# Sixteen score tiles moved forward, and one exponential moved behind a copy, in a fused attention and MLP kernel

## The chip, the cores and the metric

The kernel runs on one core of a Trainium2 chip. The metric is the device time in microseconds; the median of three runs before the change was 1639.81 us (1639.73 to 1642.65). The core has five engines with queues of their own: TensorE (PE, with its weight loads PEld), VectorE (DVE), ScalarE (ACT), GpSimd (POOL) and SyncE (SP), which here only issues DMAs. PE writes its results to PSUM, which is divided into eight banks; a tile of 128 x 512 float32 fills one bank.

## The reference

```python
xn = _layernorm(x)                                   # x: 1 x 2048 x 512
q, k, v = split(xn @ wqkv)                           # 32 heads of 16
scores = einsum("bhqd,bhkd->bhqk", q, k) * 16**-0.5
s = (softmax(scores) @ v) @ wo
g = silu(gelu(xn @ w1 + b1) @ w2 + b2)               # 512 -> 1376 -> 512
return x + s * g
```

There are 2048 tokens, a model width of 512, 32 heads of 16, and a hidden width of 1376. The inputs are float32.

## The kernel before

The products are made in float32 accuracy from two parts: an operand is split into a rounded part and a rest (names ending in h and l), and three products, hh, hl and lh, are summed in one PSUM bank.

**Units and tiles.** Attention is cut into 32 units. A unit `u` is a group of four heads (`g = u // 4`, `NG` = 8 groups) with a chunk of 512 queries (`c = u % 4`). Each unit is computed twice. The first pass makes 64 *score tiles* of 128 queries by 512 keys (`s_one`, line 165): a matmul (line 174) and a row maximum by DVE (line 176). They serve only to find each query's maximum. When a unit's 64 tiles are done, `s_end0`, `s_end1` and `s_end2` negate, transpose and store the maxima to DRAM. The second pass makes the *probability tiles*, 128 keys by 512 queries (`t_one`, line 647): a matmul (line 654) whose operands carry two additional rows, so that the maximum is subtracted within the product, and an exponential by ACT (line 656). The *value product* (`pv_step`, line 716, matmuls on line 723) accumulates 16 key blocks of a unit in one bank, and after the last one ACT copies the bank out to SBUF (the output copy, `os`, line 730).

**Three stages.** The first (to about 53 us) normalises and transposes x and computes part of the values and the queries and keys of groups 0 and 1. The queries and keys go to DRAM (`qk_h`, `qk_l`, lines 312 and 313) and come back with their rows rearranged (`load_k`, line 99, and `load_qs`, line 133).

The second stage, the *MLP stage* (to about 479 us), runs a list of parts (`plan`): the rest of the values (`quad`), the two MLP products (`half` and `down`) and the remaining queries and keys. All its matmuls contract over 64 rows, two halves of PE's rows working side by side; `run` walks through slots of two such matmuls, and `prog["n"]` counts them. Between them `fill` (line 481) puts early score tiles, by a due count that is linear in the slot number: it starts at slot `FILL0` = 84 and reaches `4 * LEAD` = 560 tiles at the last of `SLOTS` = 1470 slots. Loads for later units stand on a list, `errands`; one entry is taken at fixed places of each `half`. The weights' loads and the list's loads share SP's queue.

The third stage, the *attention stage*, is a loop of 513 steps written out by hand. Step n makes the four probability tiles T of key block n % 16 of unit n // 16, some score tiles S of later units, and the value product V of the step before. How many S there are is the difference of a due count (line 839) and the tiles already made; their place in the step is a string:

```python
ORDER = {0: "TTTTV", 1: "TTTTSV", 2: "TTTSTSV", 3: "STTTSTSV", 4: "STTSTSVTS"}
...
return min(4 * L, 4 * LEAD + max(0, (4 * (L - LEAD) * n - 300) // (DONE - 1)))
```

`L` is 512, and `DONE` = 492 is the step from which the output projection is worked in.

**Banks in the attention stage.** The four T of a step write the bank of `ps_m` and the three of `ps_t`, in that order (`t_tile`, line 639). The S use two banks of `ps_s` and a third, which alternates: `ps_v` and `ps_x` take turns as accumulator of the value product, and the one that isn't accumulating serves score tiles. At step 16u + 1 the ring of score banks is set anew: the first two S take `ps_s`, the third takes the bank of the unit that has just ended.

**Hand-over.** Step 16u holds the first four T of unit u and the last value product of unit u - 1. In the order in which ACT gets its work, the four exponentials come first and the output copy after them.

**Keys.** Three buffers hold keys (`KB` = 3). Group 3 reuses the first buffer: POOL's queue issues its loads in two halves of 1024 keys, at steps 57 and 64. Later groups are loaded piece by piece.

Of the kernel before, what the change touches and what calls it, by code (L numbers as in the profile page):

```python
# [10 lines left out]
AF = mybir.ActivationFunctionType  # L11
# [6 lines left out]
S = 2048  # L18
# [5 lines left out]
CH = 512  # L24
NCH = S // CH
# [4 lines left out]
EPS = 1e-5  # L30
SCALE = DH ** -0.5
VW = DH + 1
LEAD = 140
NW = 10
EARLY = 4
DONE = 492
FILL0 = 84
HB = 4
W2B = 2
ORDER = {0: "TTTTV", 1: "TTTTSV", 2: "TTTSTSV", 3: "STTTSTSV", 4: "STTSTSVTS"}  # L40
KB = 3
# [5 lines left out]
def fused(ctx: ExitStack, tc: tile.TileContext, x, wqk, wv, wo, w1, b1, w2, b2, out):  # L47
    nc = tc.nc
# [50 lines left out]
    def load_k(g, pieces=range(6), eng=nc.sync, c0=0, n=S):  # L99
        both = kws[g % KB]  # L100
        for i in pieces:
            a, b = divmod(i, 3)
            r, cs = slice(64 * a + DH * b, 64 * a + DH * b + DH), slice(c0, c0 + n)
            src = rows((qk_h, qk_h, qk_l)[b], g, 1, a, c0, n)
            if both is not None:
                eng.dma_start(both[r, :, cs].bitcast(F32), src)
            else:
                for p in range(2):
                    eng.dma_start(kts[g % KB][p][r, cs].bitcast(F32), src[:, p])
# [23 lines left out]
    def load_qs(u, sides=range(2)):  # L133
        if u < NU:
            QS[u] = qzs[u % 2] if u < LEAD // 16 else qss[0][:, u % 2]
            q_rows(QS[u], u, sides)

    def ask_qs(u):
        for a in range(2):
            errands.append((load_qs, u, (a,)))  # L140

    def load_qt(u):
        QT[u] = qts[u % 2]
# [9 lines left out]
    later, errands = [], []  # L153
# [11 lines left out]
    def s_one(a):  # L165
        u, st, p = halves[a][made[a]]
        made[a] += 1
        g = u // NCH
        qi, ki = divmod(st, NCH)
        if u not in MX:  # L170
            MX[u] = qring.tile([P, GH, NCH, NCH], F32, name="mx")
        ps = s_tile()
        r, q = slice(64 * a, 64 * a + 3 * DH), QS[u]
        nc.tensor.matmul(ps, q[r, p, qi * P:(qi + 1) * P],  # L174
                         kts[g % KB][p][r, ki * CH:(ki + 1) * CH], start=True, stop=True)
        nc.vector.tensor_reduce(MX[u][:, 2 * p + a, qi, ki:ki + 1], ps, axis=AX.X, op=OP.max)  # L176
        if min(made) == 32 * (ended[0] + 1):
            v = ended[0]
            ended[0] += 1
            s_end0(v)  # L180
            later.append([12 if "seen" in prog else 8, v])
# [61 lines left out]
    for j in range(len(pairs)):  # L243
        for h in range(2):
# [9 lines left out]
            n = 2 if nd < len(parts) and parts[nd][2] and ready - nd > room else 1  # L254
# [28 lines left out]
    def w2_load(i):  # L283
        if i < len(ms):
            W2[ms[i][1:]] = w_new(w2[ms[i][2]], 2, "raw2")
# [35 lines left out]
    with ExitStack() as s1:  # L321
# [54 lines left out]
        def v_tile(t):  # L376
            pv = a_tile((P, D))
            c, ts = t // NCH, slice(t % NCH * P, t % NCH * P + P)
            for k in range(KT):
                mm3(pv, (xh[c][:, k, ts], xl[c][:, k, ts]), (wv_h[:, k], wv_l[:, k]), k == 0, k == KT - 1)  # L380
            v_out(t, pv)

        def q_first(c):
            pq = {}
            for g in range(2):
                ps = pq["q", g, c] = a_tile((P, CH))
                for k in range(KT):
                    ks = slice(k * P, (k + 1) * P)
                    mm3(ps, (W1[g][0][:, ks], W1[g][1][:, ks]), (xh[c][:, k], xl[c][:, k]), k == 0, k == KT - 1)
            evac(list(pq), pq)  # L390
# [58 lines left out]
        for c in range(1, NCH):  # L449
            for t in range(NCH * c, NCH * c + NCH):  # L450
                turn(t)
            if c < NCH - 1:
                ln(NCH * c + NCH, NCH)
            else:
                nc.scalar.activation(warm[:, 1:], warm[:, :1], AF.Gelu_apprx_tanh)
                w1_load(0)
                w2_load(0)
                w2_load(1)
            v_tile(c - 1)
            q_first(c)  # L460
        v_tile(NCH - 1)

    keep_r = ctx.enter_context(tc.tile_pool(name="keep_r", bufs=1, side="right"))
    qring = ctx.enter_context(tc.tile_pool(name="qring", bufs=2, side="right"))
# [5 lines left out]
    qzp = qz.enter_context(tc.tile_pool(name="qzp", bufs=1, side="right"))  # L470
    for i in range(2):
        qzs.append(qzp.tile([P, 2, CH], F32R, name=f"qz{i}"))

    SYNC = mybir.DependencyInfo(mybir.DependencyClass.Sync, mybir.DependencyReason.DATA)
    prog.update(n=0, pe=0, seen=0)
# [141 lines left out]
    def quad(n):  # L617
        us = first[n]
        for u, b in zip(us, BANKS[n]):
            pool, name = {"x": (ps_x, "ps"), "m": (ps_m, "ps"), "v": (ps_v, "pv"), "t": (ps_t, "pst")}[b]  # L620
            PH[u] = pool.tile([P, CH], F32, name=name)
        for i in range(4):
            hooks = {6: [mark]} if i in (1, 2) else {}
            if n == VQ - 2 and i in (0, 2):
                hooks[3] = [lambda: w1_split(0) if i == 0 else w1_load(1)]
            run((terms(us[i], 0, i < 2), terms(us[(i + 2) % 4], 1, i < 2)), hooks)
            if i >= 2:
                for u in (us[i - 2], us[i]):
                    v_out(u[1] * NCH + u[2], PH.pop(u))
# [3 lines left out]
        for i in range(6):  # L633
            errands.append((load_k, g, (i,)))

    PT = {}
    turns, PN = [0], []

    def t_tile():
# [7 lines left out]
    def t_one(u, k, p, a):  # L647
        g = u // NCH
        if (u, k) not in PT:
            PT[u, k] = slot(3 + len(PN) % 3, (P, GH, CH))  # L650
            PN.append(1)
        ps = t_tile()
        r = slice(64 * a, 64 * a + 3 * DH + 2)
        nc.tensor.matmul(ps, kts[g % KB][p][r, k * P:(k + 1) * P],  # L654
                         QT[u][r, p, :], start=True, stop=True)
        nc.scalar.activation(PT[u, k][:, 2 * p + a, :], ps, AF.Exp, scale=SCALE)  # L656

    load_k(0)
    load_qs(0)
    k_ones(kts[0])  # L660
    for n, e in enumerate(plan):
        if e[0] == "half":
            half(*e[1:])
        elif e[0] == "first":
            quad(e[1])
        else:
            if e[1] == parts[-2]:
                nc.scalar.activation(mhw, ident_r[:1, :1].bitcast(F32), AF.Exp)
            if e[1] == parts[-1]:
                for i in range(EARLY):  # L670
                    t_one(0, 0, i // 2, i % 2)
            down(*e[1])
        if e == ("first", VQ - 1):
            w2_split(0)
            w2_load(2)
            ask_qs(1)
            ask_k(1)
        if e[0] == "half" and pairs[e[1]][0] == ("q", NG - 1, 0) and e[2] == 1:
            kts.append([slot(p, (P, S), F32R) for p in range(2)])
            kws.append(None)  # L680
            qss.append(slot(2, (P, 2, 2, CH), F32R))
            ask_k(2)
        if n == len(plan) - 8:
            load_qt(0)
            load_mh(0)
# [30 lines left out]
    def pv_step(u, k):  # L716
        g = u // NCH
        if k == 0:
            pool = pv_pool(u)
            PV[u] = pool.tile([P, CH], F32, name="pv" if pool is ps_v else "ps")  # L720
        for j in range(GH):
            h = (g * GH + j) * VW
            nc.tensor.matmul(PV[u][32 * j:32 * j + 32, :], vsb[:, k, h:h + 32], PT[u, k][:, j, :],  # L723
                             start=(k == 0), stop=(k == NT - 1))
        del PT[u, k]
        if k == NT - 1:
            OS[u] = wb.tile([P, CH], F32, name="os", bufs=1)
            pv = PV.pop(u)
            if u < NU - 1:
                nc.scalar.activation(OS[u], pv, AF.Copy)  # L730
            else:
                nc.scalar.activation(OS[u][:, :CH // 2], pv[:, :CH // 2], AF.Copy)
                nc.vector.tensor_copy(OS[u][:, CH // 2:], pv[:, CH // 2:])
# [103 lines left out]
    L = 16 * NU  # L837

    def due(n):
        return min(4 * L, 4 * LEAD + max(0, (4 * (L - LEAD) * n - 300) // (DONE - 1)))  # L840

    for u in range(NU):
        g, c = divmod(u, NCH)
# [33 lines left out]
    for n in range(L + 1):  # L877
        ua, ka = divmod(n, 16)
        want = due(n) - sum(made)
        i = 0  # L880
        if n > 1 and (n - 1) % 16 == 0:
            s_ring[:] = [ps_s, ps_s, pv_pool((n - 1) // 16 + 1)]
            s_turn[0] = 0
        for op in ORDER[want] if n > 1 else ("TTTTV", "TTTVTSS")[n]:
            if op == "S":
                h = 1 - last if made[1 - last] - made[last] < 4 and made[1 - last] < 2 * L else last
                s_one(h)
                last = h
            elif op == "V":
                if n:  # L890
                    pv_step(*divmod(n - 1, 16))
                for _ in range(4):
                    tick()
                flush()
            else:
                if EARLY <= 4 * n + i < 4 * L:
                    t_one(ua, ka, i // 2, i % 2)
                    last = i % 2
                for f, args in todo.get((n, i), []):
                    f(*args)  # L900
                i += 1
# [56 lines left out]
```

## Time and profile before

| | us |
|---|---|
| median of three runs (lowest to highest) | 1639.81 (1639.73 to 1642.65) |
| the profiled execution | 1640.26 |
| its span, first to last instruction | 1638.5 |
| PE busy | 1627.3 (99%) |
| DVE busy | 1389.8 (85%) |
| ACT busy | 1271.9 (78%) |
| POOL busy | 373.5 (23%) |
| first score tile of the MLP stage | 73.1 |
| first probability tile | 479.5 |

The span lies 1.8 us under the execution's own time. A row of the profile gives a line of the kernel, an engine, an operation, the tile written and the tiles read, and shapes; a start and a duration in us where it is a timeline row, or a count and durations in ns where it is a group. `PE ... x8` on one row is eight matmuls merged in order of time; each `pv_step` call appears as eight. A square bracket tells how long the engine was idle before, and what ended that. Ends of matmuls are modelled.

### The profile page before, as it was taken

To read this page: it belongs to the slowest core of one execution; us is meant where nothing else is said; L and a number is where in the kernel's file an instruction comes from. 1 tells how busy PE (TensorE), PEld (TensorE's weight loads), DVE (VectorE), ACT (ScalarE), POOL (GpSimd) and SP (SyncE) were. 2 spreads that over 40 slices of the span, in tenths; PEclk is the share of its full clock that TensorE was granted. 3 is DMA by queue.
4 is the path that set the end of the run, shared out by engine and by line. 5 is a ranking of instruction groups with operands and counts; after the bars stand their busy time and mean duration, and the time that the engine had idled before them with its cause. 6 is when DMAs were issued, how large, how long until landed. Compare 5 with 4: busy or idle time off the path is not lost.

```text
span 1638.5 us, 31026 instructions
## 1 busy us (share of the span) xinstructions
PE 1627.3 (99%) x11656; PEld 898.3 (55%) x11656; DVE 1389.8 (85%) x2299; ACT 1271.9 (78%) x2523; POOL 373.5 (23%) x366
## 2 busy tenths in 40 slices
PE   9999999999999999999999999999999999999998
PEld 7898999988974434333334443433334443434445
DVE  7299999999988888888888888888888888888733
ACT  4333433434349999999999999999999999999984
POOL 4235565756630011001000100100100000000144
PEclk9999999999999999999999999999999999999999
DMA  6625334453330122112301411411141111110152
GB/s 200 147 72 150 113 118 130 138 135 121 111 117 26 29 50 47 31 45 49 61 26 28 79 29 28 66 31 31 36 59 32 28 28 37 32 28 22 56 191 94
DMA packets 76214, 116.83 MB, mean 71 GB/s; under 512 B 24964, under 2 KB 26244, under 8 KB 74696
## 3 DMA queue, kind: packets, MB, share of 16 engines
q1 hardware_dynamic: 72604, 102.42, 22.3%
q0 software_dynamic: 3264, 12.35, 4.5%
q8 instruction: 92, 1.51, 0.4%
q14 instruction: 58, 0.48, 0.1%
q10 hardware_dynamic: 196, 0.07, 0.0%
HBM read 84.35 MB, written 25.97 MB: 67 GB/s over the span
## 4 chain that ended last, share of the span: by engine, by line
PE 94%; DVE 2%; issue 2%; ACT 1%; POOL 1%; DMA 0%; SPq 0%; ACTq 0%; DVEq 0%; POOLq 0%
PE ps L174 23%; PE pv L723 15%; PE ps L723 15%; PE ps L506 12%; PE pst L654 12%; PE pst L506 7%; PE pv L174 3%; PE ps L77 2%; PE pv L506 2%; ACT slot L656 1%; PE pst L77 1%; POOL ol L791 1%; DVE mx L176 0%; PE ps L654 0%; POOL gx L824 0%
## 5 line engine op out<-in xcount | busy, mean ns | idle before, releaser
L176 DVE TENSOR_REDUCE mx<-ps 128x1 f32<-128x512 f32 x1808 | 1168.6, 685 | 160.3 <-PE ps L654 76.6
L656 ACT ACTIVATE slot<-pst 128x512 f32<-128x512 f32 x1533 | 806.9, 608 | 5.0 <-PE ps L174 4.5
L656 ACT ACTIVATE slot<-ps 128x512 f32<-128x512 f32 x515 | 308.7, 600 | 44.4 <-PE ps L654 9.8
L174 PE MATMUL ps<-kt,slot 48*128 48x512 f32 x864 | 327.9, 443 | 0.0
L174 PEld LDWEIGHTS ps<-kt,slot 48*128 48x128 f32 x864 | 158.2, 184 | 256.8 <-DVE mx L176 235.6
L654 PE MATMUL pst<-qt,kt 50*128 50x512 f32 x1149 | 294.1, 409 | 0.4 <-DVE gt L587 0.3
L723 PE MATMUL pv<-slot,vsb 128*32 128x512 f32 x2048 | 272.7, 605 | 0.0
L723 PE MATMUL ps<-slot,vsb 128*32 128x512 f32 x2048 | 272.5, 604 | 0.0
L506 PE MATMUL ps<-slot,w1h 64*128 64x512 f32 x1088 | 225.2, 394 | 0.4 <-ACT junk L519 0.4
L174 PE MATMUL ps<-kt,qz 48*128 48x512 f32 x512 | 211.1, 416 | 0.2
L654 PE MATMUL ps<-qt,kt 50*128 50x512 f32 x387 | 189.8, 492 | 0.0
L176 DVE TENSOR_REDUCE mx<-pv 128x1 f32<-128x512 f32 x240 | 163.8, 683 | 11.6 <-PE ps L654 7.8
L174 PE MATMUL ps<-slot,slot 48*128 48x512 f32 x432 | 166.2, 441 | 0.2
L506 PEld LDWEIGHTS ps<-slot,w1h 64*128 64x128 f32 x1088 | 153.8, 185 | 9.5 <-ACT junk L519 2.3
L654 PEld LDWEIGHTS pst<-qt,kt 50*128 50x128 f32 x1149 | 144.5, 186 | 21.5 <-issue 8.4
L506 PE MATMUL ps<-slot,w1l 64*128 64x512 f32 x544 | 154.0, 393 | 0.0
L174 PEld LDWEIGHTS ps<-slot,slot 48*128 48x128 f32 x432 | 78.6, 184 | 115.0 <-DVE mx L176 104.8
L307 POOL TENSOR_TENSOR hl<-hg,hh 128x512 fp32r<-128x512 f32 x76 | 96.9, 1297 | 129.2 <-ACT hh L306 80.8
L189 POOL TENSOR_TENSOR nmh<-nm,nmh 128x16 fp32r<-128x16 f32 x32 | 7.1, 221 | 497.9 <-DVE nm L188 266.5
L519 ACT ACTIVATE junk<-ident_r 1x1 f32<-1x1 f32 x91 | 17.8, 196 | 120.4 <-PE pst L506 104.0
L174 PEld LDWEIGHTS ps<-kt,qz 48*128 48x128 f32 x512 | 93.7, 183 | 11.8 <-DVE mx L176 2.7
L654 PE MATMUL pst<-qt,slot 50*128 50x512 f32 x384 | 97.7, 406 | 0.0
(161 smaller groups left out, 1980.7 us busy)
## 6 DMA issues: line engine op xcount, KB each, us to landing
raw<-in_w SPq DMA_DIRECT2D x88, 256.0 KB
qk_h<-hh SPq DMA_DIRECT2D x32, 256.0 KB
qk_l<-hl SPq DMA_DIRECT2D x32, 256.0 KB
qt<-qk_h SPq DMA_DIRECT2D x128, 64.0 KB
slot<-qk_h SPq DMA_DIRECT2D x96, 64.0 KB
xt<-in_x SPq DMA_DIRECT2D x16, 256.0 KB
g_d<-gt POOLq DMA_DIRECT2D x16, 256.0 KB, 3.7
qt<-qk_l SPq DMA_DIRECT2D x64, 64.0 KB
```

What stands on the lines that cost most here:

```text
L77: nc.tensor.matmul(ps, lhs[a], rhs[b], start=first and n == 0, stop=last and n == 2)
L174: nc.tensor.matmul(ps, q[r, p, qi * P:(qi + 1) * P], kts[g % KB][p][r, ki * CH:(ki + 1) * CH], start=True, stop=True)
L176: nc.vector.tensor_reduce(MX[u][:, 2 * p + a, qi, ki:ki + 1], ps, axis=AX.X, op=OP.max)
L189: nc.gpsimd.tensor_sub(NM[u][:, 1], nm, NM[u][:, 0].bitcast(F32))
L307: nc.gpsimd.tensor_sub(hl, raw, hh.bitcast(F32))
L506: i = nc.tensor.matmul(ps, lhs[r], rhs[r], start=first, stop=last).ins
L519: i = nc.scalar.activation(junk[:, :1], ident_r[:1, :1].bitcast(F32), AF.Copy).ins
L654: nc.tensor.matmul(ps, kts[g % KB][p][r, k * P:(k + 1) * P], QT[u][r, p, :], start=True, stop=True)
L656: nc.scalar.activation(PT[u, k][:, 2 * p + a, :], ps, AF.Exp, scale=SCALE)
L723: nc.tensor.matmul(PV[u][32 * j:32 * j + 32, :], vsb[:, k, h:h + 32], PT[u, k][:, j, :], start=(k == 0), stop=(k == NT - 1))
L791: lo.tensor_sub(ol[:, :n], src, oh[:, :n].bitcast(F32))
```

## The change

There are five parts.

1. `LEAD` goes from 140 to 144: 576 early score tiles instead of 560, which is exactly nine units. `FILL0` goes from 84 to 50, so the fill starts 34 slots sooner. As `LEAD // 16` is now 9, the queries of units 0 to 8 use the two buffers `qz`.
2. In the attention stage the due count rises by exactly three a step, `3 * n - 1`; no step makes four score tiles, and the last are made in step 491.
3. The exponential of the fourth T in a unit's first step (which is the step of the last value product of the unit before) is held back on a list, `put_off`, and issued after the value product and its output copy. This holds for all units but the first.
4. Loads: queries of unit 0 and three quarters of group 0's keys are issued before the last values and the last q/k chunk of the first stage, the last quarter of the keys after them. `load_k(0)` and `load_qs(0)` after the definition of `t_one` are gone. `ask_qs` puts query rows at the front of `errands`, ahead of keys; unit 1's are asked for after the first `quad`.
5. In units 0, 12 and 24, the first ones on a new set of three key buffers, the score tiles go key chunk by key chunk, not query block by query block.

```diff
-LEAD = 140
+LEAD = 144
-FILL0 = 84
+FILL0 = 50
...
     def ask_qs(u):
-        for a in range(2):
-            errands.append((load_qs, u, (a,)))
+        errands[:0] = [(load_qs, u, (a,)) for a in range(2)]
...
-        qi, ki = divmod(st, NCH)
+        qi, ki = divmod(st, NCH) if u % (NCH * KB) else divmod(st, NCH)[::-1]
...
                 w2_load(1)
+                break
             v_tile(c - 1)
             q_first(c)
-        v_tile(NCH - 1)
...
+    load_qs(0)
+    load_k(0, c0=0, n=S - CH)
+    v_tile(NCH - 2)
+    q_first(NCH - 1)
+    v_tile(NCH - 1)
+    load_k(0, c0=S - CH, n=CH)
...
-        nc.scalar.activation(PT[u, k][:, 2 * p + a, :], ps, AF.Exp, scale=SCALE)
-
-    load_k(0)
-    load_qs(0)
+        dst = PT[u, k][:, 2 * p + a, :]
+        put_off.append(lambda: nc.scalar.activation(dst, ps, AF.Exp, scale=SCALE))
+        if not (k == 0 and u and p == a == 1):
+            put_off.pop()()
+
...
             quad(e[1])
+            if e[1] == 0:
+                ask_qs(1)
...
-            ask_qs(1)
             ask_k(1)
...
     def due(n):
-        return min(4 * L, 4 * LEAD + max(0, (4 * (L - LEAD) * n - 300) // (DONE - 1)))
+        return min(4 * L, 4 * LEAD + max(0, 3 * n - 1))
...
                     pv_step(*divmod(n - 1, 16))
+                while put_off:
+                    put_off.pop()()
                 for _ in range(4):
                     tick()
```

More of the change, by code (lines that the diff above doesn't have):

```diff
@@ L634, in ask_k @@
             errands.append((load_k, g, (i,)))
-    PT = {}
+    PT, put_off = {}, []
     turns, PN = [0], []
```

## The prediction

> **What bounds the kernel now.** I read the page first, then the busy time by window, then the attention stage as a timeline of PE and of ACT, and the chain of waits at one hand-over from unit to unit.
>
> ```profile
> PE 1627.3 (99%) x11656; PEld 898.3 (55%) x11656; DVE 1389.8 (85%) x2299; ACT 1271.9 (78%) x2523; POOL 373.5 (23%) x366
> 60.00:80.00 20.00, 19.64 (x171) 16.38 (x169) 6.12 (x9) 7.23 (x16) 4.64 (x4) 1.00 0.53 102
> 200.00:300.00 100.00, 99.91 (x830) 90.78 (x828) 92.02 (x144) 39.16 (x88) 62.17 (x54) 1.00 0.39 117
> 520.00:920.00 400.00, 400.00 (x2786) 160.26 (x2782) 356.96 (x599) 385.25 (x750) 38.57 (x58) 1.00 0.21 44
> L174 PE MATMUL ps<-kt,qz x512: 387/397/503, 73.1 to 441.8; 48*128 48x512 f32 x171
> L176 DVE TENSOR_REDUCE mx<-ps x1808: 626/682/694, 73.5 to 1551.8; 128x1 f32<-128x512 f32 x181
> L654 PE MATMUL ps<-qt,kt x387: 387/497/501, 479.5 to 1610.9; 50*128 50x512 f32 x194
> ```
>
> The columns of a window are span, then busy time (instructions) of PE, PEld, DVE, ACT and POOL, clock, DMA share and GB/s. PE is full in both stages, at clock 1.00. In the MLP stage (to 479.5) it passes 830 matmuls per 100 us, 0.12 us each; DVE is 92% busy. From 60 to 80 DVE is nearly idle (6.12 of 20). In the attention stage PE is full and ACT is next, 385 of 400.
>
> A step of the attention stage is the distance between two starts of the value product, line 723:
>
> ```profile
> 595.11 1.06 PE L723 MATMUL ps<-slot,vsb 128*32 128x512 f32 x8
> 597.01 1.06 PE L723 MATMUL ps<-slot,vsb 128*32 128x512 f32 x8
> 599.75 1.06 PE L723 MATMUL ps<-slot,vsb 128*32 128x512 f32 x8
> 601.88 1.07 PE L723 MATMUL ps<-slot,vsb 128*32 128x512 f32 x8
> 604.01 1.07 PE L723 MATMUL ps<-slot,vsb 128*32 128x512 f32 x8
> ```
>
> Steps of three score tiles S take 2.13 (599.75 to 601.88 to 604.01). Step 53 had four S: 595.11 to 597.01 to 599.75 is 1.90 + 2.74 = 4.64 for two steps, 0.38 over 2 x 2.13.
>
> The hand-over after a unit's last value product is the other slow place. T1 to T4 are a step's probability tiles, exp1 to exp4 their exponentials, S1 to S3 its score tiles; the order on PE is S1 T1 T2 T3 S2 T4 S3, value product.
>
> ```profile
> 897.83 0.48 PE L174 MATMUL ps<-kt,slot 48*128 48x512 f32 x1
> 898.07 0.40 PE L654 MATMUL pst<-qt,kt 50*128 50x512 f32 x1
> 898.40 1.07 PE L723 MATMUL ps<-slot,vsb 128*32 128x512 f32 x8
> 899.97 0.97 PE L174 MATMUL ps<-kt,slot 48*128 48x512 f32 x2
> 900.87 1.06 PE L723 MATMUL pv<-slot,vsb 128*32 128x512 f32 x8
> ```
> ```profile
> 898.32 1.57 ACT L656 ACTIVATE slot<-pst 128x512 f32<-128x512 f32 x3
> 899.75 0.63 ACT L730 ACTIVATE os<-ps 128x512 f32<-128x512 f32 x1
> 900.23 0.64 ACT L656 ACTIVATE slot<-ps 128x512 f32<-128x512 f32 x1
> ```
> ```profile
> 899.89 0.50 ACT os L730
> 900.39 0.04 issue
> 900.44 0.50 PE ps L174
> ```
>
> This step takes 900.87 - 898.40 = 2.47, 0.34 over 2.13. S3 writes the bank that the output copy (line 730) empties, so it starts at 900.44, 0.06 after the copy's end at 900.38; the value product follows 0.43 later. The copy stands behind exp4 on ACT; the value product it reads had ended at 899.47.
>
> **The change, part by part.** The sum is made against the profiled execution, 1640.26 us (span 1638.5), which lies 0.45 over the median of 1639.81 and inside the runs shown.
>
> *Steps of four S.* Line 840 made the due count rise 1488/491 = 3.0305 a step, so 0.0305 x 491 = 15 steps had four S. The new count rises by 3 and none is left: 15 x 0.38 = 5.7 saved, their extra tiles included. The sixteenth moved tile stood alone in step 492, in the end part, where output work makes steps of 3.2:
>
> ```profile
> 1561.12 1.06 PE L723 MATMUL pv<-slot,vsb 128*32 128x512 f32 x8
> 1564.35 1.06 PE L723 MATMUL pv<-slot,vsb 128*32 128x512 f32 x8
> ```
>
> At 0.12 for its matmul it gives 0.1.
>
> *The 16 tiles in the MLP stage.* Their matmuls cost PE 16 x 0.12 = 1.9. DVE has to reduce 16 more at 0.68 = 10.9; the fill opens at slot 50 in place of 84, and 34 slots of two matmuls at 0.12 give 8.2 us of DVE that was idle. The remaining 2.7 us spreads over 8% idle time of some 400 us. Bounds for this part: 0 (tiles fill places that PE loses beside them now) and 2.7 (DVE decides). I take 1.9, since PE is the full one.
>
> *Loads ahead of the fill.* The first S now stands at slot 53, about 34 x 0.24 = 8 us before 73.1, near 65. What it needs:
>
> ```profile
> 44.50 1.89 SPq L221 DMA_DIRECT2D raw<-in_w  x4
> 51.85 0.33 SPq L312 DMA_DIRECT2D qk_h<-hh  x1
> 55.04 0.79 SPq L106 DMA_DIRECT2D kt<-qk_h  x2
> 65.58 0.30 SPq L131 DMA_DIRECT2D qz<-qk_h  x1
> ```
>
> Queries and three quarters of the keys now issue on SP right behind the raw weights, from some 46.4. Those twelve issues and their waits took 10.8 us before (55.04 to 65.88); at that pace they are issued by 57.2, with the q/k writes of the last chunk behind them instead of at 51.85, and the last quarter of the keys (six issues) and the four rows of ones follow. The late writes feed only this last quarter, wanted at tile 48, some 48 x 0.7 us after 65. So no stall: 0. If the cover goes, PE waits at slot 53 in order, up to 5 us for one load. Query rows ahead of keys on the errand list reorder SP issues inside the same stage: 0. What PE's score loads waited for, in full (us, times), has no load in it:
>
> ```profile
>   DVE mx L176: 384.2, 467
>   ACT os L730: 8.4, 28
>   issue: 0.4, 1
>   DVE mh L208: 0.2, 1
> ```
>
> So earlier queries gain nothing, and the price of a later key is bounded by the same 5 us.
>
> *Group 3's keys.* Unit 12's tiles begin at step (768 - 576)/3 = 64, not 69. POOL issued the two halves at steps 57 and 64:
>
> ```profile
> 601.82 1.09 POOL L106 DMA_DIRECT2D kt<-qk_h  x2 [11.49 <-PE pst L654]
> 618.84 1.05 POOL L106 DMA_DIRECT2D kt<-qk_h  x2 [2.37 <-PE pst L654]
> ```
>
> Step 64 lies near 620, 15 us behind the first half's last issue. With the tiles now ordered by key chunk, the second half is wanted 32 tiles, 10.7 steps or 23 us later. 0.
>
> *exp4 behind the output copy.* This decides the sign. On ACT the order in a unit's first step becomes exp1, exp2, exp3, copy, exp4. S3 of the next step no longer waits for exp4's time ahead of the copy. But two things follow. First, the copy cannot start before the value product ends, at 899.47; exp4's own place was at 899.28 (the third of the three from 898.32, 0.48 apart), so ACT now idles. Second, T4 of the next step writes the bank exp4 empties (lines 639 to 645: four banks, the same one for the fourth tile of every step), so T4, which stands ahead of S3 and the value product, waits for exp4 behind the copy. From PE's end to ACT's start the nearest rows give:
>
> ```profile
> 901.87 0.49 PE L654 MATMUL ps<-qt,kt 50*128 50x512 f32 x1
> 902.43 0.60 ACT L656 ACTIVATE slot<-ps 128x512 f32<-128x512 f32 x1
> 1614.02 1.04 PE L723 MATMUL ps<-slot,vsb 128*32 128x512 f32 x8
> 1615.21 0.39 ACT L732 ACTIVATE os<-ps 128x256 f32<-128x256 f32 x1 [1.23 <-PE ps L723]
> ```
>
> 902.36 to 902.43 is 0.07; 1615.06 to 1615.21 is 0.15 for the last unit's copy. So the copy starts at 899.54 to 899.62, exp4 0.48 later at 900.02 to 900.10 and ends, after its 0.61, at 900.63 to 900.71; T4 starts 0.06 later and the value product 0.43 after that (S3 rides beside T4 on the other half of the rows): 901.12 to 901.20 against 900.87. Each hand-over grows by 0.25 to 0.33; I take 0.28. The next step's exponentials end 0.3 later too, but ACT has 15 of 400 idle and T4 after that stands over 2 us on, so it doesn't run on. Score tiles run at 30 hand-overs (units 1 to 30): 30 x 0.28 = 8.4. The 31st lies in the end part, with steps of 3.2 us: 0. Where the trace has no such order, the bounds are wider: the whole wait on the copy gone (8.4 us in 28 waits above, -0.30 each), and a whole ACT slot on PE, +0.48; times 30, -9 to +14.
>
> Sum: 1640.26 - 5.7 - 0.1 + 1.9 + 8.4 = 1644.76, 1644.8.
>
> **The rivals.**
>
> *PE or ACT goes around the late exponential (faster).* The rows above show S3 at 897.83 and T4 at 898.07 although T4 stands first in the program, so a matmul can pass another. If S3 and the value product could pass a T4 that waits, the gate would be the copy's end: 899.54 + 0.63 + 0.06 + 0.43 = 900.66, 0.21 less than 900.87; 30 x 0.21 = 6.3, in all 1640.26 - 5.7 - 0.1 + 1.9 - 6.3 = 1630. Against it: the passing row is of two tiles that both had their data. It decides faster when T4's wait costs less than 0.06 a hand-over. The Trainium skill, "PSUM — Partial Sum Buffer", section "Engine vs sequencer instructions", has ScalarE as a strict FIFO and matmuls starting in program order; by that rule neither exp4 passes the waiting copy nor anything T4, and the time is that of the main sum. On the start order of matmuls the trace differs by these two rows; on ACT no row here shows it either way.
>
> *The hand-over comes out even.* If the copy's 0.07 and T4's release are shorter than read (ends on PE are modelled), +0.25 shrinks to about 0, and the four-S steps decide: 1636.4. For it: a modelled end at 899.47 that is 0.2 late; against it: 0.07 at both kinds of row.
>
> *A load is late.* SP's writes of the last q/k chunk stand behind twelve loads, and PE stops at slot 53 or tile 48. Up to 5 us once, more if the raw weights slip too: 1650. Against it: 8 us between 57 and 65.
>
> **How the numbers follow.** Main case 0.72, around 1644.8, its own range 1641.5 to 1648.5; PE goes around 0.09, even hand-over 0.11, late load 0.08. A measurement tells about 0.2%, 3.3 us, from no change. Of the main case some 0.1 lies below 1643.1; the late load is all slower: slower 0.70. Half the even case and all of the passing one fall below 1636.5: faster 0.14; the rest, same 0.16. The range takes in the main case, the even hand-over and part of the late load: 1636 to 1649.
>
> **What the profile after would show.** No step of 1.90 followed by 2.74; 576 score tiles before the first line-654 matmul, the first near 65 us; that first probability tile some 2 us later than 479.5. At hand-overs, ACT idle between exp3 and the copy, released by PE; T4 waiting on ACT; the step 2.7 to 2.8 instead of 2.47. The prediction is wrong if the hand-over stays at 2.47 or falls, if PE idles at slot 53 or at the third unit's first tiles, or if the MLP stage grows by more than 3 us.

## The result and the profile after

| | before | after |
|---|---|---|
| median (us), runs taken together | 1640.56 | 1646.62 |
| lowest to highest | 1639.73 to 1642.65 | 1646.05 to 1647.27 |
| the profiled execution, its span | 1640.26, 1638.5 | 1646.9, 1645.1 |
| first score tile of the MLP stage | 73.1 | 65.6 |
| first probability tile | 479.5 | 484.8 |

The ratio is 1.0035, with a 95% interval of 1.0022 to 1.0048: the change makes the kernel slower by about a third of a per cent. The forecast was 1644.8, slower.

The first line of the page after shows the same kind of kernel, with PE full (the mean granted clock of this execution is 1.00, as before):

```profile
PE 1623.9 (99%) x11656; PEld 895.6 (54%) x11656; DVE 1392.4 (85%) x2299; ACT 1274.9 (77%) x2524; POOL 372.9 (23%) x366
```

Three places answer to those shown before. The first is the value product's starts, in the timeline of PE around step 53:

```profile
600.91 1.07 PE L731 MATMUL ps<-slot,vsb 128*32 128x512 f32 x8
603.04 1.07 PE L731 MATMUL ps<-slot,vsb 128*32 128x512 f32 x8
605.17 1.06 PE L731 MATMUL ps<-slot,vsb 128*32 128x512 f32 x8
607.30 1.07 PE L731 MATMUL ps<-slot,vsb 128*32 128x512 f32 x8
```

Each of these steps is 2.13, and no 1.90 followed by 2.74 is left in the trace. The second is the same hand-over as before (units 11 to 12), as timelines of PE and of ACT. Times are on the new scale; 904.07 answers to 898.40.

```profile
903.74 0.40 PE L660 MATMUL pst<-qt,kt 50*128 50x512 f32 x1
904.07 1.07 PE L731 MATMUL ps<-slot,vsb 128*32 128x512 f32 x8
...
905.64 0.39 PE L173 MATMUL ps<-kt,slot 48*128 48x512 f32 x1
906.34 0.50 PE L660 MATMUL pst<-qt,kt 50*128 50x512 f32 x1 [0.31 <-ACT slot L663]
906.35 0.50 PE L173 MATMUL ps<-kt,slot 48*128 48x512 f32 x1
906.77 0.64 PE L731 MATMUL pv<-slot,vsb 128*32 128x512 f32 x4
```
```profile
903.99 1.08 ACT L663 ACTIVATE slot<-pst 128x512 f32<-128x512 f32 x2
905.20 0.60 ACT L738 ACTIVATE os<-ps 128x512 f32<-128x512 f32 x1
905.70 0.59 ACT L663 ACTIVATE slot<-pst 128x512 f32<-128x512 f32 x1
906.17 0.60 ACT L663 ACTIVATE slot<-ps 128x512 f32<-128x512 f32 x1
```

The copy starts at 905.20, when the value product is over, and not at exp3's heels: exp3 started near 904.47. The late exponential runs from 905.70 to 906.29. The fourth probability tile (906.34, released by ACT) and the third score tile (906.35) start together behind it, although the bank of the third score tile was free from 905.80. The value product follows at 906.77, so the step lasts 2.70 in place of 2.47. The chain of waits shows the same, in order of time:

```profile
905.20 0.60 ACT os L738
905.80 0.50 ACT slot L663
906.30 0.04 issue
906.34 0.50 PE pst L660
```

Of the 30 hand-overs with score tiles, 29 last 2.70 to 2.71 and the first 2.75; before they lasted 2.46 to 2.49, and the last 2.31. The mean goes from 2.470 to 2.703, which makes 30 x 0.233 = 7.0 us.

The 31st hand-over (units 30 to 31) lies in the end part, where no score tiles are left and six matmuls of the output projection stand behind the fourth probability tile. It grows more, from 3.25 to 4.27. Its end before (its start, 1564.35, is a row of the prediction), and its PE and ACT rows after:

```profile
1567.60 1.06 PE L723 MATMUL ps<-slot,vsb 128*32 128x512 f32 x8
```
```profile
1570.55 1.06 PE L731 MATMUL pv<-slot,vsb 128*32 128x512 f32 x8
...
1572.82 0.49 PE L660 MATMUL pst<-qt,kt 50*128 50x512 f32 x1 [0.55 <-ACT slot L663]
...
1574.82 1.07 PE L731 MATMUL ps<-slot,vsb 128*32 128x512 f32 x8
```
```profile
1571.68 0.60 ACT L738 ACTIVATE os<-pv 128x512 f32<-128x512 f32 x1 [0.26 <-PE pv L731]
1572.17 0.59 ACT L663 ACTIVATE slot<-pst 128x512 f32<-128x512 f32 x1
```

The wait is the same: the copy waits for the value product, the late exponential for the copy, the tile for the exponential.

The third place is the MLP stage. The rows are groups (count, durations in ns, first and last start in us) for the stage's first matmuls, its score tiles and the first probability tile, and the window from 120 to 470 with the columns of the prediction's windows. Before, without the two groups that the prediction shows:

```profile
L506 PE MATMUL pst<-kt,slot x192: 384/391/495, 53.3 to 96.8; 64*128 64x512 f32 x192
120.00:470.00 350.00, 349.75 (x2891) 316.50 (x2889) 322.58 (x499) 136.17 (x309) 212.28 (x181) 1.00 0.44 128
```

After:

```profile
L512 PE MATMUL pst<-kt,slot x192: 384/391/500, 53.6 to 99.2; 64*128 64x512 f32 x192
L173 PE MATMUL ps<-kt,qz x512: 386/397/502, 65.6 to 435.4; 48*128 48x512 f32 x171
L660 PE MATMUL ps<-qt,kt x387: 388/497/502, 484.8 to 1618.1; 50*128 50x512 f32 x194
120.00:470.00 350.00, 349.76 (x2872) 316.49 (x2874) 320.78 (x497) 134.17 (x305) 210.78 (x180) 1.00 0.43 127
```

From its first matmul to the first probability tile the stage took 479.5 - 53.3 = 426.2 before and takes 484.8 - 53.6 = 431.2 now: 5.0 us more for 16 tiles, though they begin 7.5 us sooner. In a window of the same length PE passes 2872 matmuls instead of 2891.

The balance of the two spans: start 0.3, MLP stage +5.0, 30 hand-overs +7.0, the 31st +1.0, the other steps of the attention stage (whose mean goes from 2.151 to 2.138 over 459 steps) -5.7, the rest of the end part -1.0: 6.6, which is 1645.1 - 1638.5. Of the last term 0.4 lies in the two steps from the value product of step 490 to that of step 492, which last 6.05 together in place of 6.48.

### The profile page after: what moved, and what is told of

Its sections match the earlier page's. It is cut to its first block, busy times and chain, and to the rows that moved or that the text cites. A ratio compares the mean times of both kernels' runs of the same rounds, so it can differ in the third digit from the quotient of the medians.

```text
span 1645.1 us, 31017 instructions
## 1 busy us (share of the span) xinstructions
PE 1623.9 (99%) x11656; PEld 895.6 (54%) x11656; DVE 1392.4 (85%) x2299; ACT 1274.9 (77%) x2524; POOL 372.9 (23%) x366
## 4 chain that ended last, share of the span: by engine, by line
PE 95%; ACT 2%; DVE 2%; issue 0%; DMA 0%; SPq 0%; DVEq 0%; ACTq 0%
PE ps L173 23%; PE ps L731 16%; PE pv L731 16%; PE pst L660 12%; PE ps L512 12%; PE pst L512 7%; PE ps L77 3%; PE pv L173 2%; PE pv L512 2%; ACT os L738 1%; ACT slot L663 1%; PE pst L77 1%; PE ps L660 1%; PE pv L77 1%; DVE mx L175 0%; PE ps L199 0%
## 5 line engine op out<-in xcount | busy, mean ns | idle before, releaser
L173 PE MATMUL ps<-kt,slot 48*128 48x512 f32 x864 | 338.6, 447 | 0.0
L173 PE MATMUL ps<-slot,slot 48*128 48x512 f32 x368 | 145.8, 447 | 0.1
L173 PEld LDWEIGHTS ps<-slot,slot 48*128 48x128 f32 x368 | 67.3, 184 | 126.8 <-DVE mx L175 119.1
```

Source lines behind the costliest of these rows:

```text
L173: nc.tensor.matmul(ps, q[r, p, qi * P:(qi + 1) * P], kts[g % KB][p][r, ki * CH:(ki + 1) * CH], start=True, stop=True)
```

## The experiments

**The exponential back in its place.** In the changed kernel, the one edit is

```diff
-        dst = PT[u, k][:, 2 * p + a, :]
-        put_off.append(lambda: nc.scalar.activation(dst, ps, AF.Exp, scale=SCALE))
-        if not (k == 0 and u and p == a == 1):
-            put_off.pop()()
+        nc.scalar.activation(PT[u, k][:, 2 * p + a, :], ps, AF.Exp, scale=SCALE)
```

> The changed kernel with the fourth exponential back in its place ahead of the output copy; everything else stays changed. Theory H (the late exponential makes the fourth probability tile of the next step wait, 0.23 us at each of 30 hand-overs): the hand-over step goes from 2.70 back to 2.47 us and the time from 1646.6 to about 1639.6. Rival R (the longer attention stage comes from something else in the change, such as the steady three score tiles on a set ring of banks): the hand-over stays at 2.6 to 2.7 and the time stays above 1644. The first probability tile should stay at 484.8 under both, since this part does not touch the MLP stage.

Measured: 1638.63 us, ratio to the kernel before 0.9993 (0.9984 to 1.0003). The mean hand-over is 2.471, the 31st is 3.25 again, and the first probability tile is at 483.6, 430.9 after the stage's first matmul. In this trace the hand-over of units 11 to 12 reads

```profile
900.32 1.06 PE L728 MATMUL ps<-slot,vsb 128*32 128x512 f32 x8
902.80 1.07 PE L728 MATMUL pv<-slot,vsb 128*32 128x512 f32 x8
```

2.48 again. Theory H holds; the 1639.6 that it gave left out the 31st hand-over. The time is 8.0 us below that of the change, which is 7.0 for the 30 and 1.0 for the 31st. The rest of the change comes out even.

**The exponential alone,** in the kernel before: the same edit the other way round, with the `while put_off` loop behind `pv_step`.

> The kernel before with the fourth exponential put behind the output copy and nothing else. Theory H: hand-overs at 2.70 in place of 2.47, 30 x 0.23 = 7.0 us, so about 1647.5, with the first probability tile still at 479.5 and the fifteen pairs of 1.90 and 2.74 still there. Rival R: within 2 us of the kernel before.

Measured: 1648.02 us, ratio 1.0048 (1.0033 to 1.0063). The mean hand-over is 2.702, the first probability tile at 479.1, and the fifteen pairs of 1.90 and 2.74 are there. So this part alone costs the 7 us of the 30 hand-overs, and 1.0 us more at the 31st, which I had put at nothing: it lasts 4.29 here. In the three traces with the late exponential (this one, the change, and the next but one) that step takes 4.27 to 4.29, in the other eleven 3.25 or 3.26.

**The loads alone.** In the kernel of the first experiment:

```diff
-LEAD = 144
+LEAD = 140
-FILL0 = 50
+FILL0 = 84
...
-        return min(4 * L, 4 * LEAD + max(0, 3 * n - 1))
+        return min(4 * L, 4 * LEAD + max(0, (4 * (L - LEAD) * n - 300) // (DONE - 1)))
```

> The kernel before with the loads of the change alone (queries and three quarters of the keys early, query rows at the front of the list, key order in units 0, 12 and 24); 560 tiles, the fill from slot 84, the old due count, no exponential moved. It asks where the 5.4 us of the MLP stage come from. Theory P (the tiles' places among the slots and their number cost it, the loads nothing): first probability tile at 479.5 within 0.5, time 1640.5 within 1. Rival Q (early loads delay the weights or PE): first probability tile 2 to 3 us later, time about 1643.

Measured: 1640.82 us, ratio 1.0006 (0.9996 to 1.0015); the stage lasts 479.9 - 53.7 = 426.2. The loads cost nothing that can be told, and the growth of the MLP stage is with the tiles.

**The fourth probability tile behind the value product.** In the changed kernel, exponential still late:

```diff
-        for op in ORDER[want] if n > 1 else ("TTTTV", "TTTVTSS")[n]:
+        hand = n > 1 and n % 16 == 1 and want == 3
+        for op in "STTTSSVT" if hand else ORDER[want] if n > 1 else ("TTTTV", "TTTVTSS")[n]:
```

> The changed kernel, exponential still behind the copy, but in the step after each hand-over the fourth probability tile stands behind the value product (order S T T T S S V T). This takes the wait on the late exponential from in front of the value product and leaves the copy's wait on PE as it is. Theory H: the third score tile then starts after the copy alone, near 900.2 on the old trace's scale, and the value product near 900.6, so the hand-over step falls from 2.70 to about 2.25, the step after it grows by 0.1 to 0.2, and the time falls by 30 x 0.3 = 9 to about 1637. Rival R2 (it is the idle time of ACT itself that sets the step, because the exponentials of the next step come late): the two steps together stay at 2.70 + 2.13 and the time at 1646.

Measured: 1647.63 us, ratio 1.0047 (1.0032 to 1.0061), where theory H had 1637. The hand-over step fell to 2.21, as theory H said (2.25), but the next one rose to 2.66 and took it all back. Its timeline of PE tells why; 903.86 is the last value product of a unit:

```profile
903.86 1.07 PE L731 MATMUL ps<-slot,vsb 128*32 128x512 f32 x8
...
906.06 1.11 PE L731 MATMUL pv<-slot,vsb 128*32 128x512 f32 x8
907.10 0.50 PE L660 MATMUL pst<-qt,kt 50*128 50x512 f32 x1
...
908.29 0.50 PE L660 MATMUL pst<-qt,kt 50*128 50x512 f32 x1 [0.19 <-ACT slot L663]
908.29 0.50 PE L173 MATMUL ps<-kt,slot 48*128 48x512 f32 x1
908.72 0.64 PE L731 MATMUL pv<-slot,vsb 128*32 128x512 f32 x4
```

The tile moved behind the value product runs at 907.10; its exponential ends 1.1 us later; the next step's fourth tile has the same bank, waits for that, and starts at 908.29 with an engine idle before it. The wait was passed on by one step. The sum, 4.87 for two steps against 4.83, is what rival R2 gave. The wait named in the row is that of a tile on its own bank. But ACT also started the copy 0.73 us, and the moved tile's exponential 0.72 us, after the instruction before, in place of 0.48. So part of the two steps is idle time of ACT, as R2 has it, and this run does not tell the two apart.

**The third score tile behind the value product,** with the exponential ahead of the copy. In the kernel of the first experiment:

```diff
-        for op in ORDER[want] if n > 1 else ("TTTTV", "TTTVTSS")[n]:
+        hand = n > 1 and n % 16 == 1 and want == 3
+        for op in "STTTSTVS" if hand else ORDER[want] if n > 1 else ("TTTTV", "TTTVTSS")[n]:
```

> The changed kernel with the fourth exponential ahead of the output copy again (as in e1_no_put_off) and, in the step after each hand-over, the third score tile behind the value product (order S T T T S T V S). Theory H says the hand-over step of the old order lasts 2.47 us for one reason, the third score tile's wait on the copied bank (score tile 0.06 us after the copy's end); the fourth probability tile's bank comes free some 0.5 us sooner. So the step falls from 2.47 to 2.0 or 2.1, the next one grows by 0.1 to 0.2 as it takes the tile up, and the time is 30 x 0.25 = 7.5 below e1_no_put_off, about 1631. In e5_t4_behind_value the tile put behind the value product was one of a bank that is written again in the next step and its wait went on to that step; the third score tile's bank has a whole ring turn, so the wait should not go on. If it does go on, the two steps stay at 4.60 together and the time at 1638.6.

Measured: 1642.00 us, ratio 1.0014 (1.0004 to 1.0023). The hand-over step is 1.98, as expected, but the next is 2.70, together 4.69 against 4.60 (2.47 + 2.13). The time missed the expected 1631 by 11 us and is longer than with the old order (1638.6). ACT's timeline over both:

```profile
901.94 1.57 ACT L662 ACTIVATE slot<-pst 128x512 f32<-128x512 f32 x3
903.37 0.63 ACT L735 ACTIVATE os<-ps 128x512 f32<-128x512 f32 x1
903.84 0.65 ACT L662 ACTIVATE slot<-ps 128x512 f32<-128x512 f32 x1
904.32 1.64 ACT L662 ACTIVATE slot<-pst 128x512 f32<-128x512 f32 x3
905.75 0.70 ACT L662 ACTIVATE slot<-ps 128x512 f32<-128x512 f32 x1
```

ACT starts an instruction every 0.48 us from 901.94 on without a gap. The three exponentials that start at 904.32 end at 905.96, and PE's fourth tile of the next step, which writes the bank of the last of them, starts at 906.01. Nine instructions, eight exponentials and a copy, take 9 x 0.48 = 4.3 us of two steps that last 2 x 2.13 = 4.26 without a hand-over. So the 2.47 is not the third score tile's wait alone; ACT stands right behind it. Why the two steps take 4.69 and not 4.3 is not shown.

**Where the MLP stage's 5 us come from.** Five kernels vary the number of early tiles and the slot at which they start. The edits are of `FILL0` alone in four of them: 84 and 58 in the kernel of the last experiment (576 tiles), 50 and 40 in that of the loads alone (560 tiles).

```diff
-FILL0 = 50
+FILL0 = 84
```

> As e4_s3_behind_value, but the 576 tiles of the MLP stage start at slot 84 and not 50 (denser, same number). Read: the stage's length from its first matmul to the first probability tile, 426.2 us before and in both runs with 560 tiles, 430.9 to 431.3 in all runs with 576 tiles from slot 50. Theory N (the number of tiles costs, about 0.31 us each, wherever they stand): 431. Theory E (the early places, among the value matmuls, cost more): 426.2 + 16 x 0.15 = 428.7. Theory V (DVE, 10.9 us more work in a window that is not longer): 434 or more, since the early start is gone.

> As e4_s3_behind_value, with the fill from slot 58. Eight slots are nothing to DVE and little to the density; what changes is which slot each tile falls into. Theories N, E and V all give 431 within 0.4. Theory F (the cost hangs on which slots the tiles fall into, among the pairs of matmuls and their waits across the two halves of the rows): a length that is off 431 by 1 us or more, in either direction.

> As e3_loads_alone (560 tiles, old attention stage), but the fill starts at slot 50 and not 84, so the tiles stand farther apart. Theory N: stage length 426.2. Theory E: 428 to 429. Theory V: 426 or less.

> As e7_560_from_50, the fill from slot 40. Theory V: 34 slots earlier gave 426.2 - 423.9 = 2.3 us, so ten more slots give about 0.7: stage 423.2, time about 1637. Against it: the keys may not have landed when the first tile comes near 62 us; then PE waits in order and the stage grows by the wait, 1 to 3 us.

The fifth has 568 tiles from slot 50, otherwise as 560 from 50:

```diff
-LEAD = 140
+LEAD = 142
```

> As e7_560_from_50 with 568 tiles (LEAD 142): half the step from 560 to 576. Theory V: the stage grows by half of 7.3 us, to 427.5, and eight steps of four tiles fewer, 8 x 0.38 = 3.0, come off the attention stage: about 1638.4, no better than 560.

The last column comes from no run but from the `fill` rule in the source: how often a tile is placed four slots or less behind the last but one. The times 1637.78, 1643.89 and 1646.59 are of a single run each.

| tiles, first slot | tiles a slot | stage, us | time, us | two tiles on within four slots |
|---|---|---|---|---|
| 560 from 40 | 0.392 | 422.7 | 1636.85, ratio 0.9979 (0.9970 to 0.9988) | 7 |
| 560 from 50 | 0.394 | 423.9 | 1637.78; 1639.00 in the timed experiment below | 7 |
| 568 from 50 | 0.400 | 422.3 | 1634.04, ratio 0.9963 (0.9950 to 0.9977) | 8 |
| 560 from 84 (before) | 0.404 | 426.2 | | 36 |
| 576 from 50 (the change) | 0.406 | 431.2 | | 47 |
| 576 from 58 | 0.408 | 432.7 | 1643.89 | 62 |
| 576 from 84 | 0.416 | 436.1 | 1646.59 | 108 |

The times are of kernels that differ in the attention stage too (576 from 58 and from 84 have the third score tile behind the value product); the stage is what compares. Theory N (a fixed price per tile) fails: 568 tiles take 1.6 us less than 560 from the same slot. Theory E fails: starting earlier never costs. Theory V had 576 from 84 right (436.1 against "434 or more") and 560 from 50 and from 40 (423.9 against "426 or less", 422.7 against 423.2); for slot 58 I put it at 431 where its own price for eight slots, 8/34 of 4.9 = 1.2, would have given 432.4, near the 432.7 that came; and it is wrong by 5 us on 568 tiles (427.5 against 422.3). Theory F, that the slots into which tiles fall decide, is the one that all rows allow, but it names no length, and the last column does not explain everything either: it has 568 tiles level with 560 from slot 50, and the stage is 1.6 us shorter. The window of 568 tiles:

```profile
L512 PE MATMUL pst<-kt,slot x192: 384/391/495, 52.9 to 97.9; 64*128 64x512 f32 x192
L660 PE MATMUL ps<-qt,kt x387: 387/497/501, 475.2 to 1604.2; 50*128 50x512 f32 x194
120.00:470.00 350.00, 349.04 (x2932) 325.12 (x2930) 332.13 (x503) 137.07 (x312) 213.51 (x182) 1.00 0.43 128
```

and that of 576 from 84:

```profile
120.00:470.00 350.00, 349.70 (x2836) 318.23 (x2835) 321.74 (x502) 132.72 (x301) 207.72 (x177) 1.00 0.43 124
```

DVE has nearly the same number of instructions in all four windows, 497 to 503, while PE's matmuls go from 2836 to 2932: the same rate of score tiles, at a different cost in PE's other work. 568 tiles over 1420 slots is two in five slots exactly, and the rule then places nearly all of them (550 of 566) five slots behind the last but one.

**More work for DVE.** To ask whether DVE's rate as such holds the stage up, a small instruction was added behind every fourth early tile, in the kernel of the first experiment:

```diff
+        if "seen" in prog and sum(made) % 4 == 0:
+            nc.vector.memset(junk_v, 0.0)
...
+    junk_v = keep_r.tile([1, 1], F32, name="junk_v")
```

> As e1_no_put_off, with one more instruction on DVE, a memset of one element, behind every fourth score tile of the MLP stage: 144 of them. The profile's own one-partition memset shows 0.06 us, its one-element copies 0.14 us. PE's work is unchanged. Theory V (DVE's turn-around of the two score banks sets the rate at which tiles go through): the stage grows from 431.2 us by 144 x 0.06 to 0.14 = 9 to 20 us. If PE's own work sets it (theories N, E and F), DVE's idle time takes the memsets up and the stage stays within 1 us of 431.2.

Measured: 1639.61 us in a single run; the stage lasts 484.9 - 53.2 = 431.7, which is 0.5 more than after the change and 0.8 more than in the kernel that was edited (430.9). The memsets are there, 8.5 us of them:

```profile
L177 DVE MEMSET junk_v<- 1x1 f32 x144 | 8.5, 59 | 0.0
```

So DVE had room for at least this much on the average, and theory V, which had 9 to 20 us, falls. What is left of DVE is the moment: where three tiles come within four slots, the third may need a bank that DVE has not emptied yet. In the traces, 73 of 560 score matmuls before, 90 of 576 after and 173 of 576 (from slot 84) start within 0.1 us of the end of the reduction that frees their bank; with 560 from 50 it is 40 and with 568 it is 35.

The traces also give a price for such a start. Take the stretch from the start of the fourth matmul ahead of a score tile to the start of the fourth behind it, with no other score tile in it. It lasts 0.94 to 0.95 us on the average in all four traces below when the tile starts later than that, and more when it starts within 0.1 us:

| trace | stretch with a tile within 0.1 us, us (count) | other stretches, us (count) | more |
|---|---|---|---|
| 568 from 50 | 1.107 (34) | 0.940 (513) | 0.167 |
| before | 1.080 (53) | 0.947 (455) | 0.133 |
| after | 1.075 (72) | 0.950 (441) | 0.125 |
| 576 from 84 | 1.052 (128) | 0.946 (331) | 0.106 |

By an estimate from these rows, seven MLP matmuls at 0.115 leave some 0.14 us for a tile that starts later, and all starts within 0.1 us cost 73 x 0.133 = 9.7 us before, 90 x 0.125 = 11.3 after and 173 x 0.106 = 18.3 from slot 84. With 16 x 0.14 = 2.2 for the tiles, this makes some 4 of the 5.0 us. The estimate is rough: from the change to 576 tiles from slot 84 it gives 7 us, and 4.9 were measured. The number of helper instructions by which ACT releases one half of PE's rows to the other (`junk`) is no rival: it is 90 to 93 in all seven traces. That crowding is the whole price is not shown: no run holds the number of tiles and the start and changes the crowding alone.

**The first version that was faster, timed.**

> The kernel of e7_560_from_50 again, timed: the kernel before with the loads of the change and the fill from slot 50, 560 tiles, the old due count, no exponential moved. Its one time was 1637.78. Theory V: 2.3 us below the kernel before, 1637.5 against 1639.8, a ratio of 0.9986.

Measured: 1639.00 us, ratio 0.9994 (0.9985 to 1.0003), with a stage of 423.9 again. The gain of the stage repeats, 2.3 us; that of the whole kernel is too small to tell from nothing. The version with 568 tiles, at 1634.04, beats both kernels and lies 4 us below the 1638.4 that was expected. Against the kernel before, 3.8 us come from the MLP stage, and the steps that are no hand-overs, with fewer steps of four score tiles among them, take 2.8 us less.

## Why the prediction was right, and where it was off

- *Sign and place.* The hand-over decided, by the path that was worked out: the copy waited for the value product, the late exponential for the copy, the fourth tile for its bank, the value product for that tile. Putting the exponential back took 8.0 us away, and putting it late in the kernel before added 8.
- *Size of the hand-over.* Forecast 0.28, measured 0.233, 7.0 us instead of 8.4. At units 11 to 12 the copy began 1.13 after the value product's start (1.14 to 1.22 forecast), the exponential 0.50 after the copy (0.48), and it took 0.59 (0.61); the fourth tile followed after 0.05 (0.06), the value product after 0.43 (0.43). Most of the error is the wait ahead of the copy, where the 0.15 of the last unit's copy did not come.
- *The 31st hand-over* was put at nothing, because the end part has steps of 3.2 us. That a step is long gave no room: PE sat idle for 0.55 us and the six projection matmuls behind the tile came later with it, so the late exponential cost 1.0 us in one step.
- *Steps of four.* 15 x 0.38 = 5.7 forecast, 5.7 measured. The sixteenth tile, taken out of the end part, was put at 0.1; the end part without its hand-over got shorter by 1.0, of which 0.4 lies in two steps near that tile and the cause of the rest is not shown. That this 1.0 cancels the one of the 31st hand-over is luck.
- *The MLP stage* is the mis-sized term: 1.9 forecast with bounds of 0 and 2.7, 5.0 measured. The prediction called itself wrong if this stage grew by more than 3 us, and on this term it was. The step that failed is "PE is the full one, 0.12 a matmul". 0.12 us is what PE spends per matmul on the average of the stage; a score tile costs more than a matmul among its like. The 172 MLP matmuls ahead of the first score tile before (53.3 to 73.1) run at 0.115, so the tiles of before cost (426.2 - 2976 x 0.115) / 560 = 0.15 each on the average, with the 2976 MLP-stage matmuls of the trace. At that price 16 tiles make 2.4. The rest of the 5.0 is in part, by the estimate from the traces above, that more tiles started just behind a reduction; what makes up the remainder stays open. The bound from DVE spread its work over the 8% of idle time of the stage; the memsets show that there was such room on the average, and the starts just behind a reduction show that it was not there at each tile's moment.
- *Loads and keys.* No wait showed at slot 53, at tile 48 or at unit 12, and the loads alone cost nothing that can be told. The queries and three quarters of the keys were issued by 54.8 (57.2 forecast), the last quarter from 64.5, well ahead of tile 48 at 99.9. No run shows the 5 us that were put on one late load.
- *Rivals.* PE did not go around the waiting tile: the third score tile, with its bank free from 905.80, started at 906.35, beside the tile that stood ahead of it. By the Trainium skill, "PSUM — Partial Sum Buffer", section "Engine vs sequencer instructions", ScalarE's queue is a strict FIFO; the trace after agrees, since the late exponential's matmul had ended by 904.14 (903.74 + 0.40), and it ran at 905.70 behind the copy. The even hand-over and the late load did not come.
- *The total.* The 30 hand-overs were forecast 1.4 too high, the MLP stage 3.1 too low, and the end part's two errors of about 1 cancel. So the forecast of 1644.8 is nearer to 1646.6 than its terms are to theirs; the sign rests on the hand-over, which was understood, the nearness in part on luck.

## What to carry to other kernels

Before an instruction that waits is put ahead of another on an in-order queue, list who needs what stands behind it: here a copy that frees one bank was put ahead of an exponential that frees a bank wanted even sooner, and the wait only changed its name. A long step is no reason to put a new wait in it at nothing; look at what stands behind the waiting instruction. When work is interleaved by a due count, how often places crowd counts beside their number; of the kernels here, the one with a ratio of two in five had the shortest stage, by 0.4 us. And price an inserted piece by runs with more and fewer of it in the same stage, not by the stage's average per instruction.

## What was unexpected of the hardware

A score tile's cost in the MLP stage is no constant: seven kernels with 560 to 576 tiles spread over 422.3 to 436.1 us, and the one with 568 is the shortest. The same late exponential cost 0.23 us in a step with three score tiles and 1.02 in the one with six projection matmuls. At a hand-over three limits stand within a few tenths of a microsecond: the copied bank, the fourth tile's bank, and ACT's nine instructions at 0.48 us in two steps. Taking either tile out from in front of the value product shortened that step to 2.21 or 1.98 us, and the next step grew to 2.66 or 2.70.
